# Second tile of a fused retention and expert kernel: the fifth block's transposes between the fourth block's two output passes, VectorE's fence, later weight sums and another order of PSUM banks

## The chip, the cores and the metric

The kernel runs on one core of a Trainium2 chip. The metric is the device time of one execution in microseconds; the times of before are three executions with a median of 293.08 us (292.98 to 293.34).

## The reference

Inputs are q, k and v of shape 8 x 8 x 576 x 64 (batch, head, position, width), and two weight matrices of 512 x 2048 and 2048 x 512. Cut to what matters:

```python
scores = np.matmul(q, k.transpose(0, 1, 3, 2)) / np.sqrt(64)
gamma = 1.0 - 2.0 ** (-5.0 - np.arange(8))           # one per head
rel = pos[:, None] - pos[None, :]
ret = scores * np.where(rel >= 0, gamma ** rel, 0.0)
x = np.matmul(ret, v)                                # to 4608 tokens x 512
h = x @ w_in
out = (h * np.cos(h)) @ w_out                        # 4608 x 512, float32
```

## The kernel before

**Blocks and tiles.** The 4608 tokens are 18 blocks of 256. Two blocks make a tile of 512 tokens, so there are nine tiles, n = 0 to 8. The second tile (n = 1) holds blocks 2 and 3; in the code a block is `j`, counted from 0. So the "fourth block" of the title is j = 3 and the "fifth" is j = 4.

**The retention part of a block.** GpSimd scales q and k by powers of gamma (`prep`, line 203, tile `qks`) and rounds v (`round_v`, line 214, tile `vb`). TensorE transposes q and k (`turned`, line 239), and ScalarE or VectorE copies the two transposed halves to SBUF (line 245, tile `qkT`). TensorE makes the scores (`scores`, line 332), VectorE masks them (line 341, tile `ret`). TensorE sums the states (`sums_of`, line 365), VectorE adds them up (line 416), and ScalarE rounds them (line 425, tile `sb`). Then `outputs(j, bank)` makes the block's slice of x in a PSUM tile `ov`: `out_own` multiplies masked scores by v in two passes (line 449), `out_carried` adds what comes from earlier states (line 477), and ScalarE copies the result to `xT` (line 496).

**The fence.** The two passes of `out_own` write the same PSUM regions from different halves of TensorE's rows. Between them stands either a drain of TensorE (no `guard` given) or a one-element copy on ScalarE that waits for the first pass and that the second pass waits for (line 464); in the second form TensorE does the work of `guard()` meanwhile.

**The expert part of a tile.** `mm1` does x times w_in in eight steps i = 0 to 7 for n = 1. A step is 16 matmuls of 128x256 into a PSUM tile `h` of one bank pair (line 525), a cosine on ScalarE into `cosh` (line 538, two buffers), and a multiplication on VectorE that reads both `h` and `cosh` and writes `gT` (line 539). A bank pair is free for its next user once that multiplication has read it. Below, "multiplication i" is the one of step i.

**PSUM.** There are three bank pairs `m`, `a`, `b`, and two single banks `n`, `st`. The string `banks_of[1]` names the pair of each of the eight steps. Other work takes pairs by tag.

**The second matmul.** It uses sums of quarters of the weights and of gT, seven products instead of eight (`product`, `mm2_seven`, line 640). Four sums of quarters of w_out are made once, on VectorE, in half tiles (`w_sums`, line 557); sum 7 is written over a quarter of `w_out_sb` itself. The sums of gT (`g_sum`, line 579) are made on VectorE and GpSimd. For n = 1 the first product (x = 1) is made early, right after the matmuls of step 3, and after a quarter of its 16 matmuls it calls `early()`, which is `outputs(3, ...)`.

**Order.** The schedule is by hand: each engine runs its instructions in the order in which the program emits them. `mm1` takes a table `inside` of work to emit ahead of its group of four matmuls with that number. In the second tile, steps 3 and 4 emit on VectorE: two half sums of weights (6 and 4), multiplication 3, two half sums (7), the copy of half of block 4's transposes, multiplication 4. GpSimd prepares blocks 4, 5 and 6 one after the other (`step`, emitted at steps 0 and 1).

Of the kernel before, what the change touches and what calls it, by code (L numbers as in the profile page):

```python
# [17 lines left out]
def kernel(  # L18
# [9 lines left out]
    nc = tc.nc  # L28
# [13 lines left out]
    E2 = ET // 2  # L42
# [387 lines left out]

    held = []

    def out_own(j, ps, guard=None):

        ret = tiles["ret", j]
        vb = tiles["vb", j]
        begun = set()
        gate = rest = None
        if chunks[j][0].pair:
            order = [(c, y) for c in chunks[j] for y in range(2)]  # L440
        else:
            order = [(c, c.y) for c in chunks[j]]
        for swap in (1, 0):
            for hg in range(0, HG, 2):
                for c, y in order:
                    he = c.half ^ swap
                    for h in (head(he, hg), head(he, hg + 1)):
                        part = (h % 2, he)
                        i = nc.tensor.matmul(  # L449
                            ov_cols(c, ps, h, c.n),  # L450
                            lhsT=vb[c.rows, y, h, :],
                            rhs=ret[c.rows, he, h % HG, y, :],
                            start=part not in begun,
                            stop=False,
                            skip_group_check=True,
                        )
                        if gate is not None:
                            after(i, gate)
                            gate = None
                        begun.add(part)  # L460
            if swap and guard is None:
                nc.tensor.drain()
            elif swap:
                gate = nc.scalar.copy(flag[:, 1:], flag[:, :1])
                after(gate, i)
                while held:
                    held.pop(0)()
                rest = guard()
        return rest or ()
# [19 lines left out]
            tiles["x", n] = xp.tile([P, DG, W], BF16, tag="xT", name="xT")  # L489
        return tiles["x", n][:, :, j % 2 * BK : j % 2 * BK + BK]  # L490

    def outputs(j, bank, guard=None):
        ps = psum.tile([P, DG, BK], F32, tag=bank, name="ov")
        rest = out_own(j, ps, guard)
        out_carried(j, ps)
        nc.scalar.copy(x_of(j), ps)  # L496
        for run in rest:
            run()
# [12 lines left out]
    def mm1(n, et, c0, w, bank, inside={}):  # L511
        if ("g", n) not in tiles:
            tiles["g", n] = gp.tile([P, ET, W], BF16, tag="gT", name="gT")
            tiles["g", n, "done"] = 0
        gT, xT = tiles["g", n], tiles["x", n]
        m = 1024 // w
        ps = psum.tile([P, m, w], F32, tag=bank, name="h")
        steps = [(j, dg) for j in range(m) for dg in range(DG)]
        in_parts = (n, et, c0) in ((0, 0, 0), (0, 4, 0))
        if in_parts:  # L520
            steps.sort(key=lambda u: u[1] // 2)
        for u, (j, dg) in enumerate(steps):
            if u % DG == 0 and u // DG in inside:
                inside[u // DG]()
            nc.tensor.matmul(  # L525
                ps[:, j, :],
                lhsT=w_in_sb[:, dg, (et + j) * P : (et + j + 1) * P],
                rhs=xT[:, dg, c0 : c0 + w],
                start=dg == 0 and not (in_parts and w < 512 and j % 2),
                stop=dg == DG - 1,  # L530
                skip_group_check=in_parts,
            )
            spread(n, w)
        if m in inside:
            inside[m]()

        cosh = cosp.tile([P, m, w], F32, tag="cosh", name="cosh")
        nc.scalar.activation(cosh, ps, ACTF.Sin, bias=half_pi, scale=1.0)  # L538
        nc.vector.tensor_mul(gT[:, et : et + m, c0 : c0 + w], ps, cosh)  # L539

    w_sum = {}
# [66 lines left out]
    def product(n, x, early=None):  # L608
        gT = tiles["g", n]
        parts = [(j, 0, N2) for j in range(2)]  # L610
        fold = n in (1, last)
        fresh = x not in ((6, 7, 3) if fold else (6, 7))
        if fresh:
            tag = {1: "n", 2: "st", 4: "m" if n == 1 else "st", 5: "st", 3: "n"}[x]
            if x == 5 and n == last:
                tiles["o", x] = [
                    psum.tile([P, c], F32, tag=t, name="o")
                    for t, c in (("b", N2), ("m", N2 // 2), ("a", N2 // 2))
                ]
            else:  # L620
                ps = psum.tile([P, 2, N2], F32, tag=tag, name="o")
                tiles["o", x] = [ps[:, j] for j in range(2)]
                tiles["all", x] = ps
        if x in (5, 3) and n == last:
            parts = [(0, 0, N2), (1, 0, N2 // 2), (1, N2 // 2, N2)]
        dst = tiles["o", x if fresh else 5 if x == 3 else 1]
        lhs = {1: gT[:, :E2, :256], 2: gT[:, E2:, :256], 4: gT[:, E2:, 256:]}.get(x)
        if lhs is None:
            lhs = tiles["gs", n, x]
        rhs = {1: w_quarter(0, 0), 2: w_quarter(1, 0), 3: w_quarter(1, 1)}.get(x)  # L630
        if rhs is None:
            rhs = w_sum[x]
        order = [(e, i) for e in range(E2) for i in range(len(parts))]
        if len(parts) > 2:
            order.sort(key=lambda u: u[1])
        for u, (e, i) in enumerate(order):
            if early and u == len(order) // 4:
                early()
            j, c0, c1 = parts[i]
            nc.tensor.matmul(  # L640
                dst[i],
                lhsT=lhs[:, e, j * P : (j + 1) * P],
                rhs=rhs[:, e, c0:c1],
                start=(fresh and e == 0 and (i == 0 or len(parts) > 2)),
                stop=(e == E2 - 1 and (i == len(parts) - 1 or len(parts) > 2)),
                skip_group_check=True,
            )
        return parts
# [279 lines left out]
        0: [(0, 0, BK), (0, BK, BK)] + [(et, 0, W) for et in range(4, ET, 2)],  # L928
        1: [(et, 0, BK) for et in range(0, ET, 4)] + [(et, BK, BK) for et in (8, 0, 12, 4)],
    }  # L930
    banks_of = {0: "mbambamb", 1: "mabmbmab", 2: "abmabmab"}

    adds, ps1 = [], []

# [17 lines left out]

    stores = []

    for n in range(NT):
        blocks = blocks_of.get(n) or [(e + k * E2, 0, W) for e in range(0, E2, 2) for k in range(2)]
        for i, (et, c0, cw) in enumerate(blocks):
            inside = {
                (0, 0): {2: block1_outputs},
                (1, 0): {2: lambda: w_sums(4, 0, 4), 4: lambda: states_and_scores(3, None, ("n", "st"))},  # L960
                (1, 1): {4: lambda: adds.append(sums_of(3, ("n", "st"))())},
                (1, 3): {1: lambda: (adds.pop()(), w_sums(6, 4, E2), w_sums(4, 4, E2))},
                (1, 4): {2: lambda: turned(4, ("st", "a"), (act, vec))},
                (1, 7): {2: lambda: turned(5, "m")},
                (2, 0): {1: lambda: adds.append(sums_of(6, ("n", "st"))())},
                (2, 1): {1: lambda: adds.pop()()},
                (2, 5): {1: lambda: turned(7, ("n", "st"))},
            }.get((n, i), {})
            mm1(n, et, c0, cw, banks_of.get(n, turn_of(n) * 3)[i], inside)
            if (n, i) == (1, 0):  # L970
                step(False)
                load_next()
            if (n, i) == (1, 1):
                step(False)
                for r0, ot in stores[3:] + stores[:3]:
                    stored_rows(r0, 0, DM, ot)
                load_next()
                step()
            if (n, i) == (1, 3):
                w_sums(7, 0, 4)  # L980
                w_sums(7, 4, E2)
                mm2_seven(1, {}, None, (1,), lambda: outputs(3, "a"))
            if n:
                sums_after(n, i)
            if n == 2 and i in (2, 4):
                for y in range(2):
                    scaled(nc.gpsimd, 8, "q" if i == 2 else "k", y)
            if (n, i) == (2, 6):
                round_v(8)
                prepared = 9  # L990
                load_next()
                load_next()
# [68 lines left out]
        def first_scores(flush, pend):  # L1061
            g_sum(n, 5, 4, E2)
            six = g_sum(n, 6, 4, E2)
            masks = scores(a, "a")
            add_a = sums_of(a, "b")
            add_b = sums_of(b, "m")
            masks[0]()
            add_a()()
            masks[1]()
# [5 lines left out]

        def next_scores(flush, pend):
            masks = []
            outputs(a, "a", lambda: masks.extend(scores(b, "b")))
            for masked in masks:
                masked()  # L1080
            tiles["rounded"]()
# [3 lines left out]
            pass  # L1085

        def last_outputs(flush, pend):
            outputs(b, "a", lambda: turned(6, "m", later=True))
            flush()

        def mid_unit(flush, pend):
# [61 lines left out]
```

## Time and profile before

| | |
|---|---|
| median of three runs | 293.08 us (292.98 to 293.34) |
| profiled execution, its time | 292.63 us |
| its span on the core | 290.9 us |
| TensorE matmul busy | 284.3 us, 98% of the span |
| VectorE, ScalarE, GpSimd busy | 75%, 59%, 51% |
| granted TensorE clock | 1.00 |

The span runs from the first to the last instruction of the profiled execution; 1.7 us of its time lie around it. Timeline rows give a start and a duration in microseconds from the start of the span, the engine, the source line, what is written and read, how many instructions are merged, and in brackets the idle time before them with what ended it. PE is TensorE's matmuls, PEld its weight loads, DVE VectorE, ACT ScalarE, POOL GpSimd.

### The profile page before, as it was taken

How to read it: one execution, taken by the hardware profiler on the slowest of the kernel's cores; microseconds unless marked ns; L12 is line 12 of the kernel's file. 1: busy time of each engine (PE TensorE's matmuls, PEld its weight loads, DVE VectorE, ACT ScalarE, POOL GpSimd, SP SyncE). 2: the span in 40 equal slices, each digit the busy share in tenths (PEclk: the TensorE clock that was granted, in tenths of full speed). 3: DMA queues.
4: the chain of work that ended last, by engine and by line, in shares of the span. 5: the costliest groups of instructions: out<-in, count | busy, mean ns of one | idle time of the engine just before them, and what ended most of it. 6: DMA issues, size and time to landing. Idle time of an engine off the chain costs nothing.

```text
span 290.9 us, 10529 instructions
## 1 busy us (share of the span) xinstructions
PE 284.3 (98%) x4336; PEld 191.3 (66%) x4336; DVE 218.5 (75%) x309; ACT 170.7 (59%) x200; POOL 147.9 (51%) x169
## 2 busy tenths in 40 slices
PE   7999999999999999999999999999999999999994
PEld 2664446888854786478647874687458845884584
DVE  5767758999967967896789677977698669745943
ACT  6756216756677655676467746673767476536620
POOL 7840435698977993379136923593348024002400
PEclk9999999999999999999999999999999999999999
DMA  7999999997997989837690589139101220122013
GB/s 218 275 171 205 252 235 247 224 220 195 223 224 183 268 207 230 210 78 176 170 227 15 129 200 217 42 99 231 38 0 41 65 49 0 41 51 59 0 38 108
DMA packets 103853, 42.62 MB, mean 146 GB/s; under 512 B 68480, under 2 KB 103296, under 8 KB 103808
## 3 DMA queue, kind: packets, MB, share of 16 engines
q1 hardware_dynamic: 99104, 37.37, 52.5%
q0 software_dynamic: 4256, 4.19, 9.1%
q8 instruction: 36, 0.59, 0.8%
q10 hardware_dynamic: 448, 0.39, 0.4%
q14 instruction: 9, 0.07, 0.1%
HBM read 36.70 MB, written 9.44 MB: 159 GB/s over the span
## 4 chain that ended last, share of the span: by engine, by line
PE 94%; DVE 3%; DMA 1%; issue 0%; ACT 0%; DVEq 0%; ACTq 0%
PE h L525 43%; PE o L640 34%; PE o L1025 5%; PE ov L449 3%; PE tr L239 3%; PE ov L477 2%; PE sc L332 2%; DVE ret L312 1%; PE st L365 1%; DMA fk<-in_k_dram 1%; DVE qks L171 1%; PE sc L299 0%; PE tr L260 0%; ACT ot L670 0%; PE idle L270 0%
## 5 line engine op out<-in xcount | busy, mean ns | idle before, releaser
L525 PE MATMUL h<-xT,w_in_sb 128*128 128x512 bf16 (+1 forms) x656 | 127.4, 353 | 0.0
L539 DVE TENSOR_TENSOR gT<-h,cosh 128x1024 bf16<-128x1024 f32 x72 | 87.8, 1221 | 27.3 <-ACT cosh L538 26.8
L538 ACT ACTIVATE cosh<-h,half_pi 128x1024 f32<-128x1024 f32 x72 | 80.2, 1115 | 40.7 <-PE h L525 40.7
L525 PEld LDWEIGHTS <-w_in_sb 128*128 128x128 bf16 x656 | 63.5, 98 | 58.6 <-DMA w_in_sb<-in_moe_w_in_dram 0.2
L579 POOL TENSOR_TENSOR gs<-gT 128x512 bf16<-128x512 bf16 x30 | 38.1, 1271 | 99.6 <-DVE gT L539 99.0
L640 PEld LDWEIGHTS <-gs 128*128 128x128 bf16 x528 | 49.6, 98 | 5.9
L203 POOL TENSOR_TENSOR qks<-fk,gkc 128x512 bf16<-128x512 f32 x32 | 39.0, 1237 | 5.1 <-DMA fk<-in_k_dram 5.1
L640 PEld LDWEIGHTS <-gT 128*128 128x128 bf16 x384 | 36.6, 98 | 6.1
L666 DVE TENSOR_TENSOR ot<-ot,o 128x512 f32<-128x512 f32 x35 | 23.3, 683 | 20.2 <-ACT ot L670 12.6
L245 ACT COPY qkT<-tr 128x1024 bf16<-128x1024 bf16 x29 | 27.7, 1021 | 12.0 <-PE tr L239 11.0
L203 POOL TENSOR_TENSOR qks<-fq,gq 128x512 bf16<-128x512 f32 x28 | 31.2, 1134 | 4.6 <-DMA fq<-in_q_dram 4.6
L640 PE MATMUL o<-w_out_sb,gs 128*128 128x256 bf16 (+1 forms) x264 | 30.7, 270 | 0.0
L640 PE MATMUL o<-w_out_sb,gT 128*128 128x256 bf16 x256 | 30.6, 273 | 0.0
L640 PE MATMUL o<-ws,gs 128*128 128x256 bf16 (+1 forms) x264 | 30.4, 269 | 0.0
L670 ACT COPY ot<-o 128x512 f32<-128x512 f32 x33 | 19.2, 586 | 18.1 <-PE o L640 17.5
L341 DVE TENSOR_TENSOR ret<-sc,mask_c 128x512 bf16<-128x512 f32 x32 | 20.6, 683 | 7.5 <-PE sc L332 6.6
L214 POOL CAST vb<-fv 128x512 bf16<-128x512 f32 x35 | 22.0, 650 | 6.7 <-DMA fv<-in_v_dram 6.7
L425 ACT CAST sb<-s_all 128x768 bf16<-128x768 f32 (+2 forms) x17 | 15.6, 919 | 14.0 <-DVE s_all L416 13.9
L416 DVE TENSOR_TENSOR s_all<-st,s_all 128x256 f32<-128x256 f32 x49 | 20.7, 422 | 1.9 <-PE st L365 0.6
L496 ACT CAST xT<-ov 128x1024 bf16<-128x1024 f32 x16 | 16.2, 1012 | 9.6 <-PE ov L477 9.4
L579 DVE TENSOR_TENSOR gs<-gT 128x512 bf16<-128x512 bf16 (+1 forms) x24 | 15.8, 660 | 0.6
L579 DVE TENSOR_TENSOR gs<-gs,gT 128x1024 bf16<-128x1024 bf16 x16 | 15.2, 948 | 0.3
(83 smaller groups left out, 213.7 us busy)
## 6 DMA issues: line engine op xcount, KB each, us to landing
out_dram<-ot SPq DMA_DIRECT2D x68, 128.0 KB, 2.7
fk<-in_k_dram SPq DMA_DIRECT2D x28, 256.0 KB, 5.3
fv<-in_v_dram SPq DMA_DIRECT2D x28, 256.0 KB, 4.8
fq<-in_q_dram SPq DMA_DIRECT2D x12, 512.0 KB, 5.0
w_out_sb<-in_moe_w_out_dram POOLq DMA_DIRECT2D x4, 512.0 KB, 9.6
fq<-in_q_dram SPq DMA_DIRECT2D x4, 384.0 KB, 7.3
fk<-in_k_dram SPq DMA_DIRECT2D x2, 512.0 KB, 5.0
fv<-in_v_dram SPq DMA_DIRECT2D x2, 512.0 KB, 5.9
```

Of the source, the lines that this page charges most:

```text
L203: return eng.tensor_tensor(out=dst.rearrange("p b a d -> p a b d"), in0=src.rearrange("p (a b) d -> p a b d", a=2), in1=by.rearrange("p (a ...
L214: runs[y](vb[:, y], f[:, :, y, :] if j < NP_B else f[:, y])
L245: lambda r=r: evacs[r](tiles["qkT", j][:, :, :, :, r * HP : r * HP + HP], pss[r])
L341: nc.vector.tensor_tensor(out=ret[:, he].rearrange("p b y i -> p (b y) i"), in0=ps[he].rearrange("p b y i -> p (b y) i"), in1=mask_c.unsqu ...
L416: nc.vector.tensor_tensor(out=s32[:, u], in0=ps[c.half][:, c.y], in1=s32[:, u - 1] if u else tiles["run"], op=ALU.add,)
L525: nc.tensor.matmul(ps[:, j, :], lhsT=w_in_sb[:, dg, (et + j) * P : (et + j + 1) * P], rhs=xT[:, dg, c0 : c0 + w], start=dg == 0 and not (i ...
L538: nc.scalar.activation(cosh, ps, ACTF.Sin, bias=half_pi, scale=1.0)
L539: nc.vector.tensor_mul(gT[:, et : et + m, c0 : c0 + w], ps, cosh)
L579: i = eng.tensor_tensor(out=tiles["gs", n, x][:, e : e + step], in0=a[:, e : e + step], in1=b[:, e : e + step], op=op_,)
L640: nc.tensor.matmul(dst[i], lhsT=lhs[:, e, j * P : (j + 1) * P], rhs=rhs[:, e, c0:c1], start=(fresh and e == 0 and (i == 0 or len(parts) > 2)),
L666: return lambda: nc.vector.tensor_tensor(out=out_, in0=in0, in1=in1, op=ALU.add)
L670: held.append(lambda ps=tiles["all", x]: nc.scalar.copy(t, ps))
```

## The change

All of it concerns the second tile (n = 1).

1. `outputs(3)` is given a guard: the 32 transposes of block 4, which stood in the middle of step 4, now stand between the two output passes, in place of the drain. The fence between the passes is a one-element copy on VectorE.
2. The early product, and with it `outputs(3)`, is emitted between the cosine and the multiplication of step 3. TensorE's order stays (matmuls of step 3, then the product); on VectorE the fence comes ahead of multiplication 3.
3. VectorE's copy of block 4's second transposed half, and after it the four half sums of weights (6, 4, 7, 7), are emitted after multiplication 3.
4. Step 4 goes from pair `b` to `m`, step 5 from `m` to `b`, step 7 from `b` to `m`. `outputs(3)` goes from `a` to `b`. The later users of `m` and `b` in this tile (block 5's and 6's transposes, product 4, two sums of states, the scores of block 5) change places with each other.

```diff
-    def out_own(j, ps, guard=None):
+    def out_own(j, ps, guard=None, fence=None):
...
             elif swap:
-                gate = nc.scalar.copy(flag[:, 1:], flag[:, :1])
+                gate = fence(flag[:, 1:], flag[:, :1])
...
-    def outputs(j, bank, guard=None):
+    def outputs(j, bank, guard=None, fence=nc.scalar.copy):
         ps = psum.tile([P, DG, BK], F32, tag=bank, name="ov")
-        rest = out_own(j, ps, guard)
+        rest = out_own(j, ps, guard, fence)
...
         nc.scalar.activation(cosh, ps, ACTF.Sin, bias=half_pi, scale=1.0)
+        if "cosine" in inside:
+            inside["cosine"]()
         nc.vector.tensor_mul(gT[:, et : et + m, c0 : c0 + w], ps, cosh)
...
-            tag = {1: "n", 2: "st", 4: "m" if n == 1 else "st", 5: "st", 3: "n"}[x]
+            tag = {1: "n", 2: "st", 4: "b" if n == 1 else "st", 5: "st", 3: "n"}[x]
...
-    banks_of = {0: "mbambamb", 1: "mabmbmab", 2: "abmabmab"}
+    banks_of = {0: "mbambamb", 1: "mabmmbam", 2: "abmabmab"}
...
+    def third_outputs():
+        def turn():
+            copies = turned(4, ("st", "a"), (act, vec), later=True)
+            adds.append(copies.pop())
+            return copies
+
+        outputs(3, "b", turn, vec)
...
-                (1, 3): {1: lambda: (adds.pop()(), w_sums(6, 4, E2), w_sums(4, 4, E2))},
-                (1, 4): {2: lambda: turned(4, ("st", "a"), (act, vec))},
-                (1, 7): {2: lambda: turned(5, "m")},
+                (1, 3): {
+                    1: lambda: adds.pop()(),
+                    "cosine": lambda: mm2_seven(1, {}, None, (1,), third_outputs),
+                },
+                (1, 7): {2: lambda: turned(5, "b")},
...
             if (n, i) == (1, 3):
-                w_sums(7, 0, 4)
+                adds.pop()()
+                for x in (6, 4, 7):
+                    w_sums(x, 4 if x < 7 else 0, 4 if x == 7 else E2)
                 w_sums(7, 4, E2)
-                mm2_seven(1, {}, None, (1,), lambda: outputs(3, "a"))
...
-            add_a = sums_of(a, "b")
-            add_b = sums_of(b, "m")
+            add_a = sums_of(a, "m")
+            add_b = sums_of(b, "b")
...
-            outputs(a, "a", lambda: masks.extend(scores(b, "b")))
+            outputs(a, "a", lambda: masks.extend(scores(b, "m")))
...
-            outputs(b, "a", lambda: turned(6, "m", later=True))
+            outputs(b, "a", lambda: turned(6, "b", later=True))
```

## The prediction

> **What bounds the kernel now.** I read the page first: TensorE is busy for 98% of the span, and the chain that ended last lies 94% on it. So a microsecond that TensorE loses or wins in the second tile is one of the end, unless TensorE waits later anyway; the view of waits puts only two waits down to its matmuls, 1.3 and 0.5 us in all.
>
> ```profile
> PE 284.3 (98%) x4336; PEld 191.3 (66%) x4336; DVE 218.5 (75%) x309; ACT 170.7 (59%) x200; POOL 147.9 (51%) x169
> PE 94%; DVE 3%; DMA 1%; issue 0%; ACT 0%; DVEq 0%; ACTq 0%
> ```
>
> Next the timeline of TensorE around the fourth block's outputs.
>
> ```profile
> 55.30 0.60 PE L640 MATMUL o<-w_out_sb,gT 128*128 128x256 bf16 x4
> 55.83 0.74 PE L449 MATMUL ov<-ret,vb 64*64 64x64 bf16 x32
> 56.39 0.43 PE L477 MATMUL ov<-qkT,sb 64*64 64x64 bf16 x32
> 56.75 1.48 PE L640 MATMUL o<-w_out_sb,gT 128*128 128x256 bf16 x12
> 58.07 1.04 PE L525 MATMUL h<-xT,w_in_sb 128*128 128x256 bf16 x8
> 59.04 0.64 PE L239 MATMUL tr<-ident,qks 64*128 64x64 bf16 x32
> 59.61 5.41 PE L525 MATMUL h<-xT,w_in_sb 128*128 128x256 bf16 x48
> 64.96 0.64 PE L239 MATMUL tr<-ident,qks 64*128 64x64 bf16 x32
> ```
>
> The step's 48 matmuls run from 59.61 to 64.96; less some 0.1 for the change of form, one is 0.1095 us. So step 4 ends at 60.49, step 5 at 62.24, step 6 at 63.99. Then the timelines of VectorE and GpSimd for the same stretch.
>
> ```profile
> 53.80 2.35 DVE L539 TENSOR_TENSOR gT<-h,cosh 128x1024 bf16<-128x1024 f32 x2
> 56.06 1.41 DVE L557 TENSOR_TENSOR ws<-w_out_sb,ws 128x1024 bf16<-128x1024 bf16 x2
> 57.39 1.22 DVE L539 TENSOR_TENSOR gT<-h,cosh 128x1024 bf16<-128x1024 f32 x1
> 58.52 2.85 DVE L557 TENSOR_TENSOR w_out_sb<-w_out_sb 128x1024 bf16<-128x1024 bf16 x2
> 61.30 0.68 DVE L245 COPY qkT<-tr 128x1024 bf16<-128x1024 bf16 x1
> 61.90 1.21 DVE L539 TENSOR_TENSOR gT<-h,cosh 128x1024 bf16<-128x1024 f32 x1
> 63.59 1.23 DVE L539 TENSOR_TENSOR gT<-h,cosh 128x1024 bf16<-128x1024 f32 x1 [0.48 <-ACT cosh L538]
> ```
>
> ```profile
> 57.22 2.15 POOL L203 TENSOR_TENSOR qks<-fq,gq 128x512 bf16<-128x512 f32 x2 [2.22 <-DMA fq<-in_q_dram]
> 59.34 2.94 POOL L203 TENSOR_TENSOR qks<-fk,gkc 128x512 bf16<-128x512 f32 x2
> 62.23 1.16 POOL L214 CAST vb<-fv 128x512 bf16<-128x512 f32 x2
> ```
>
> What the reader is to see: VectorE has no gap from 53.80 to 63.1. Two weight sums took 1.41 us together at 56.06, while GpSimd stood idle for fq; two of the same size took 2.85 at 58.52, beside GpSimd, whose second pair took 2.94 instead of the 2.04 that the same two take at 51.62. They take turns, one behind the other. Multiplication 4 ends at 61.90 + 1.21 = 63.11, and step 7, which uses its bank pair, begins at 63.99: a slack of 0.88 us.
>
> **The drain and the transposes (a gain).** Without a guard, 0.56 us lie from the first output pass to the carried part (55.83 to 56.39), and the transposes inside step 4 cost 0.57 plus the change of form of 0.1: 1.23 in all. The form that comes in their place stands in the trace at 77.69: first pass, 32 transposes at 77.94, second pass at 78.51, carried part at 78.66: 0.97. Gain 0.26 us.
>
> **The fence.** At 77.69 ScalarE's fence began 0.43 us behind the first pass's start and took 0.19; the second pass came 0.82 behind that start, so 0.2 are to spare. VectorE's one-element copy isn't in the trace; bounds are its memset of 128x1 (0.06) and ScalarE's 0.19, and below nothing is excluded, as it adds an instruction. Either hides behind the transposes, so nothing is put down for TensorE; if that cover were gone, 0.1 to 0.2. On VectorE, multiplication 3 is queued behind the fence, and behind that all else.
>
> **Bank b for outputs(3) (a loss).** Pair a had been released by multiplication 1 at about 55.0. Pair b is released by multiplication 2, which starts at 54.93 and ends at 56.15. From VectorE's end to a waiting matmul 0.05 us passed at 16.20 to 16.25 (ret L312 to ov L449). The first pass thus starts at 56.20 instead of 55.83: 0.37 lost (bounds 0.3 to 0.5). So TensorE has 56.20 + 0.97 for the passes + 0.36 for the carried part + 1.32 for the other 12 product matmuls = 58.85 for step 4, which now runs unbroken for 16 x 0.1095 = 1.75 to 60.60. That is 0.11 us later than before, and step 7 is due at 64.10.
>
> **VectorE's new order.** From 56.06:
> - The fence starts at 56.20 + 0.43 = 56.63. The cosine of step 3 (55.70, 1.12 long) ends at 56.82, so multiplication 3 goes from 56.87 and hands on at 58.0 (a step of 1.13 from one multiplication to the next, as 53.80, 54.93, 56.06).
> - The copy of transposes takes 0.60 to the next (61.30 to 61.90): 58.6. Its transposes are done by 57.0.
> - Four weight sums. Free of GpSimd they take 0.65 each (56.06 to 57.39): 61.2. All four in turns with it 1.46 each: 64.4. Row by row: GpSimd is in its second q instruction (58.34 to 59.34), then two of k, then two casts. The first sum meets what the sum of before met at 58.52, whose successor started at 59.85; the second ends like that one's successor, at 61.30. The third waits for the second k instruction, which ended at 62.28, then 0.6: 62.9. The fourth either follows at once (63.5) or lets one cast of 0.55 through (64.0). The nearest row is a cast at 69.93 that took 1.12 us, against 0.61 for its neighbour at 68.95, beside a sum of gT on VectorE at 69.88: casts take turns too. I take 64.0.
> - Multiplication 4 then runs from 64.0 to 65.2, against 61.90 to 63.11. Of the 2.1 us, 0.75 is VectorE's wait around the fence and 1.3 the two sums that had lain in GpSimd's idle time.
>
> The Trainium skill (SBUF — State Buffer, "Who interferes with whom") says that a VectorE instruction with two SBUF inputs and any GpSimd instruction that reads SBUF shut each other out for a whole instruction, the later one waiting. It speaks against this change: by it the fourth sum waits for a cast as well, as in my sum; were only GpSimd's two-input instructions shut out, the sum would be half a microsecond lower. The 2.85 against 1.41 us here agrees with it.
>
> **Who waits for multiplication 4.** Step 7, due at 64.10, gets pair m from it at 65.25: 1.15 lost. Half a step and the change of form (0.97) bring TensorE to block 5's transposes at 66.22; they need pair b, released by multiplication 5, which starts at 65.13 and ends at 66.35. So they start at 66.40 against 64.96: 1.44 us later in all. Block 5's transposes waited for multiplication 5 before too, in pair m; only its time has moved.
>
> **What costs nothing.** Step 4 in pair m needs multiplication 3 (58.1) by 58.85. Step 5 in b needs ScalarE's copy of x (about 57.6 to 58.6) by 60.6; step 6 in a needs the copied transposes (58.7) by 62.4. Product 4, both sums of states and the scores keep their predecessors under the other letter. At the tile's end block 6's transposes leave b instead of m: ScalarE's two copies end at 82.02, and the next tile's step 1 in b begins at 82.98, so 0.96 to spare. No DMA and no instruction of GpSimd is emitted elsewhere; GpSimd's casts are pushed by some 0.6 us and it has 0.67 idle before 64.06. Behind step 7 VectorE and ScalarE are as late as TensorE, so nothing gives the time back.
>
> **The sum.** Profiled time 292.63 + 0.11 + 1.15 + 0.18 = 294.07. The median of the runs is 0.45 above the profiled execution: 294.5.
>
> **Rivals.**
> - *The sums don't collide.* If they run at 0.65 each behind multiplication 3, multiplication 4 ends by 62.5, no step waits, and 0.11 remains: 293.2, no change. It decides from the point at which multiplication 4 ends before 64.1, so if the four sums together take under about 4.3 us. For it: GpSimd starts after a DMA, and a later fq moves the collision. Against it: GpSimd's five instructions stand back to back from 57.22 to 63.39. Chance 0.14.
> - *The gain alone.* If pair b comes free in time for 55.83 and the sums run free, the 0.26 is left, and with a cheaper switch of forms at most 0.6: 292.5 to 292.8. Against it: VectorE's queue up to multiplication 2 is untouched. Chance 0.10, half of it beyond 0.2%.
> - *Worse turns.* Each sum takes 1.53, the longest of the rows, and the fence holds the second pass by 0.2 besides: multiplication 4 ends at 65.9, the end is 2.2 us later: 295.3. Chance 0.08.
> - The forecast, 294.0 to 295.0: 0.68.
>
> **How the numbers follow.** The likeliest is 294.5. The range goes down to the first rival with its bounds (293.0) and up to 295.2; it leaves out the gain alone and most of the worst. About 0.2% (0.6 us) is what a measurement of this kernel can tell from no change. Slower by more: 0.68 + 0.08 and a little of the first rival, 0.78. Within: 0.16. Faster: 0.06.
>
> **What would show it.** In the profile of after: the first output pass starts at about 56.2 behind multiplication 2, with idle time ended by VectorE; no drain; the fence under the transposes; the four weight sums at a mean over 1.2 us, one after another from 58.6; multiplication 4 at about 64; a wait of TensorE of about 1.15 us before step 7 for line 539, and block 5's transposes at about 66.4. The prediction is wrong if the sums' mean is near 0.7, if step 7 starts by 64.3, or if TensorE's delay at block 5's transposes has shrunk by the next tile.

## The result and the profile after

The changed kernel takes 293.94 us (median of 15 runs, 292.65 to 295.23), the kernel before 292.98 (15 runs beside them, 292.28 to 293.98). The ratio is 1.0037 with a 95% interval of 1.0021 to 1.0053: slower by 0.6 to 1.6 us, about 1.0. The profiled execution took 293.94 us, with a span of 292.2.

Line numbers of the changed kernel are two higher from line 539 on: 541 is the multiplication, 559 the weight sums, 642 the second matmul, 581 the sums of gT. First TensorE's timeline, as it was shown for before:

```profile
55.55 0.60 PE L642 MATMUL o<-w_out_sb,gT 128*128 128x256 bf16 x4
56.45 0.32 PE L449 MATMUL ov<-ret,vb 64*64 64x64 bf16 x16 [0.30 <-DVE gT L541]
56.70 0.64 PE L239 MATMUL tr<-ident,qks 64*128 64x64 bf16 x32
57.27 0.32 PE L449 MATMUL ov<-ret,vb 64*64 64x64 bf16 x16
57.42 0.43 PE L477 MATMUL ov<-qkT,sb 64*64 64x64 bf16 x32
57.78 1.49 PE L642 MATMUL o<-w_out_sb,gT 128*128 128x256 bf16 x12
59.10 5.40 PE L525 MATMUL h<-xT,w_in_sb 128*128 128x256 bf16 x48
65.05 1.03 PE L525 MATMUL h<-xT,w_in_sb 128*128 128x256 bf16 x8 [0.54 <-DVE gT L541]
66.18 0.64 PE L239 MATMUL tr<-ident,qks 64*128 64x64 bf16 x32
...
67.64 1.91 PE L642 MATMUL o<-w_out_sb,gT 128*128 128x256 bf16 x16
```

Two brackets are new, and both name the multiplication: one before the first output pass (pair b, multiplication 2), one before step 7 (pair m, multiplication 4). The early product starts 0.25 us later than in the profile of before, ahead of anything that was changed: VectorE's scaling of block 3 waits for fq until 45.57 there, until 45.32 in before. So I measure by stretches. From the early product to product 2 it was 55.30 to 66.42 = 11.12 us before and is 55.55 to 67.64 = 12.09 now: 0.97 lost. From product 2 to the next tile's first matmul (80.78 before, 82.37 after) it was 14.36 and is 14.73. Then VectorE's and GpSimd's timelines:

```profile
54.05 2.35 DVE L541 TENSOR_TENSOR gT<-h,cosh 128x1024 bf16<-128x1024 f32 x2
56.82 0.15 DVE L464 COPY flag<-flag 128x1 f32<-128x1 f32 x1 [0.42 <-PE ov L449]
57.10 1.23 DVE L541 TENSOR_TENSOR gT<-h,cosh 128x1024 bf16<-128x1024 f32 x1
58.24 0.68 DVE L245 COPY qkT<-tr 128x1024 bf16<-128x1024 bf16 x1
58.84 2.13 DVE L559 TENSOR_TENSOR ws<-w_out_sb,ws 128x1024 bf16<-128x1024 bf16 x2
60.89 2.97 DVE L559 TENSOR_TENSOR w_out_sb<-w_out_sb 128x1024 bf16<-128x1024 bf16 x2
63.79 2.34 DVE L541 TENSOR_TENSOR gT<-h,cosh 128x1024 bf16<-128x1024 f32 x2
```

```profile
59.18 2.69 POOL L203 TENSOR_TENSOR qks<-fq,gq 128x512 bf16<-128x512 f32 x2 [1.00 <-DMA fq<-in_q_dram]
61.83 2.93 POOL L203 TENSOR_TENSOR qks<-fk,gkc 128x512 bf16<-128x512 f32 x2
```

VectorE is idle between multiplication 2 and the fence. The four weight sums follow in one row from 58.84 to 63.79, 4.95 us, beside GpSimd's four scalings of block 5, which are long too. Only then comes multiplication 4, at 63.79.

### The profile page after: what moved, and what is told of

Read it like the earlier page. It is cut to its first block, busy times and chain, and to the rows that moved or that the text cites. A ratio compares the mean times of both kernels' runs of the same rounds, so it can differ in the third digit from the quotient of the medians.

```text
span 292.2 us, 10509 instructions
## 1 busy us (share of the span) xinstructions
PE 283.1 (97%) x4315; PEld 191.2 (65%) x4336; DVE 219.6 (75%) x310; ACT 170.5 (58%) x200; POOL 148.4 (51%) x169
## 4 chain that ended last, share of the span: by engine, by line
PE 86%; DVE 7%; DMA 4%; ACT 1%; issue 1%; DVEq 0%; ACTq 0%
PE h L525 39%; PE o L642 34%; PE ov L449 3%; PE tr L239 3%; PE o L1038 3%; DMA fq<-in_q_dram 2%; DVE gT L541 2%; DVE ret L312 1%; PE sc L332 1%; PE ov L477 1%; DMA fk<-in_k_dram 1%; PE st L365 1%; ACT cosh L538 1%; DVE qks L171 1%; DVE w_out_sb L559 1%
```

## The experiments

Each kernel below the first two rows ran 12 times, but the one with GpSimd held only three times. Every ratio is against the kernel before run on the same chip beside it (median 293.29 us in the first four experiments, 293.03 in the next four, 292.91 in the last three). "First stretch" is from the early product to product 2, "second stretch" from there to the next tile, both in the profiled execution, of which there is one for each kernel; most times in the text are from it.

| kernel | median us | ratio, 95% interval | first stretch | second stretch |
|---|---|---|---|---|
| before | 292.98 | | 11.12 | 14.36 |
| changed | 293.94 | 1.0037 (1.0021 to 1.0053) | 12.09 | 14.73 |
| early sums | 292.84 | 0.9991 (0.9972 to 1.0010) | 11.22 | 14.36 |
| pair a | 293.86 | 1.0028 (1.0005 to 1.0051) | 12.27 | 14.37 |
| pair a, early sums | 292.72 | 0.9983 (0.9965 to 1.0000) | 10.95 | 14.36 |
| before, sums later | 294.59 | 1.0042 (1.0021 to 1.0062) | 12.90 | 14.82 |
| pair a, early sums, ScalarE's fence | 293.11 | 1.0000 (0.9978 to 1.0022) | 11.15 | 14.72 |
| before, early sums | 293.17 | 1.0005 (0.9987 to 1.0023) | 11.12 | 14.56 |
| changed, GpSimd held | 294.98 | 1.0062 (1.0036 to 1.0088) | 11.34 | 15.71 |
| pair a, early sums, other slot | 293.27 | 1.0001 (0.9985 to 1.0017) | 10.95 | 14.56 |
| pair a, early sums, GpSimd's order | 292.90 | 0.9994 (0.9977 to 1.0011) | 11.32 | 14.36 |
| before, GpSimd's order | 292.87 | 1.0000 (0.9980 to 1.0019) | 11.24 | 14.49 |
| changed, GpSimd's order | 293.93 | 1.0029 (1.0010 to 1.0048) | 12.14 | 14.36 |

### The weight sums made earlier

```diff
-                    (2, 5, 0), (8, 5, 4), (19, 6, 0),
+                    (2, 5, 0), (8, 5, 4), (19, 6, 0), (48.5, 6, 4),
...
-                (1, 0): {2: lambda: w_sums(4, 0, 4), 4: lambda: states_and_scores(3, None, ("n", "st"))},
+                (1, 0): {2: lambda: (w_sums(4, 0, 4), w_sums(4, 4, E2)), 4: lambda: states_and_scores(3, None, ("n", "st"))},
...
-                for x in (6, 4, 7):
-                    w_sums(x, 4 if x < 7 else 0, 4 if x == 7 else E2)
+                w_sums(7, 0, 4)
```

> The changed kernel, with the second halves of weight sums 6 and 4 made earlier: 6 in tile 0 while VectorE waits for fq (a gap of 0.69 us before 45.3), 4 in step 0 of the second tile behind its first half (a gap of 0.57 before 49.7). The same computation in another order. Theory (the sums behind multiplication 3, in turns with GpSimd, make multiplication 4 late, and step 7 waits for it): the two half sums that took 2.13 us at 58.84 are gone from there, multiplication 4 starts at 61.6 to 62.0, step 7 doesn't wait, block 5's transposes wait under 0.1; the wait of the first output pass for pair b stays at 0.3 to 0.4. Against the kernel before: +0.1 us (0.0 to +0.3). Rival (the loss is pair b's wait and VectorE's idle time around the fence; the sums don't matter): step 7 still waits 0.5 or more, and the loss stays at 0.7 to 1.0 us.

TensorE's and VectorE's timelines of that kernel:

```profile
56.59 0.32 PE L449 MATMUL ov<-ret,vb 64*64 64x64 bf16 x16 [0.31 <-DVE gT L541]
...
59.24 6.28 PE L525 MATMUL h<-xT,w_in_sb 128*128 128x256 bf16 x56
65.45 0.64 PE L239 MATMUL tr<-ident,qks 64*128 64x64 bf16 x32
```

```profile
58.97 2.20 DVE L559 TENSOR_TENSOR w_out_sb<-w_out_sb 128x1024 bf16<-128x1024 bf16 x2
62.34 1.23 DVE L541 TENSOR_TENSOR gT<-h,cosh 128x1024 bf16<-128x1024 f32 x1 [1.17 <-ACT cosh L538]
```

Step 7's half runs on from step 6 (56 matmuls in one row), and multiplication 4 now waits 1.17 us for its cosine instead of coming late. The wait for pair b stayed at 0.31. The first stretch is 11.22, 0.10 above before, where 0.11 had been the term for TensorE ahead of step 7. The loss is gone (interval from -0.8 to +0.3 us). The theory holds; the rival would have kept a wait before step 7.

### The output passes in pair a

```diff
-            copies = turned(4, ("st", "a"), (act, vec), later=True)
+            copies = turned(4, ("st", "b"), (act, vec), later=True)
...
-        outputs(3, "b", turn, vec)
+        outputs(3, "a", turn, vec)
```

> The changed kernel, with outputs(3) in pair a and the second half of block 4's transposes in pair b (the two letters change places). Theory: the first pass no longer waits for multiplication 2 (0.3 us of idle time gone; the transposes may wait up to 0.1), so step 7 is due about 0.3 us earlier; but multiplication 3 is held by its cosine and not by the fence, the sums behind it stand where they stood, multiplication 4 ends when it did, and step 7 waits 0.3 longer. Against the kernel before: +0.8 to +1.1 us, as the changed kernel. Rival (pair b's wait is a loss of its own that adds to the rest): 0.3 us of the loss are gone, +0.5 to +0.7 us.

TensorE's timeline, then VectorE's:

```profile
56.14 0.32 PE L449 MATMUL ov<-ret,vb 64*64 64x64 bf16 x16
...
65.29 1.03 PE L525 MATMUL h<-xT,w_in_sb 128*128 128x256 bf16 x8 [0.99 <-DVE gT L541]
```

```profile
56.52 0.15 DVE L464 COPY flag<-flag 128x1 f32<-128x1 f32 x1
57.16 1.23 DVE L541 TENSOR_TENSOR gT<-h,cosh 128x1024 bf16<-128x1024 f32 x1 [0.49 <-ACT cosh L538]
```

The first pass starts with no idle time, 0.53 us behind the early product as in before. But multiplication 3 waits for its cosine just the same, and step 7 waits 0.99 instead of 0.54. What was won in front is given back there: the first stretch is 12.27 against 12.09. So the two waits do not add up; the later one hides the earlier one. The ratio, 1.0028, fits that, but its interval (+0.15 to +1.5 us) would fit the rival's +0.5 to +0.7 as well: only the profile speaks against the rival.

### Both

The edits of the two kernels above together.

> Both edits of the two runs before. Theory: neither wait is left, and what remains is the gain of the drain and of the form change, 0.26 us less up to 0.1 for transposes that wait for pair b: -0.15 to -0.3 us against the kernel before. Rival (the drain in fact cost little, or VectorE's fence holds the second pass): 0.0 to +0.2 us, with idle time before the second pass.

```profile
59.08 6.28 PE L525 MATMUL h<-xT,w_in_sb 128*128 128x256 bf16 x56
```

The first stretch is 10.95, 0.17 below before: neither wait is left in it, and step 7's half follows step 6 in one row. The time is lower by 0.5 us, with an interval that ends at no difference. The theory's stretch is seen, the gain in time is not clear of zero.

### The sums alone, in the kernel before

```diff
-                (1, 3): {1: lambda: (adds.pop()(), w_sums(6, 4, E2), w_sums(4, 4, E2))},
+                (1, 3): {1: lambda: adds.pop()()},
...
             if (n, i) == (1, 3):
+                w_sums(6, 4, E2)
+                w_sums(4, 4, E2)
                 w_sums(7, 0, 4)
```

> The kernel before, with one part of the change alone: the half sums 6 and 4 emitted behind multiplication 3 (and before the two of 7). Drain, place of the transposes and bank pairs as before. Theory: multiplication 3 is at 56.9 (its cosine), the four sums take 4.9 to 5.4 us from 58.0 as they stand beside GpSimd, multiplication 4 ends at 64.7 to 65.2, step 7 (in pair b, which multiplication 4 releases) waits 0.6 to 1.2: +0.7 to +1.3 us against the kernel before. Rival (the loss comes from bank pair and fence): nothing, 0.0 to +0.2 us.

```profile
64.32 2.78 PE L525 MATMUL h<-xT,w_in_sb 128*128 128x256 bf16 x24 [1.62 <-DVE qkT L245]
```

The later place of the sums is enough to make the kernel of before slower, by 0.6 to 1.8 us. The place where it hurts was a miss: VectorE's copy of the transposes stands behind the sums in this kernel, so step 6, which needs pair a from that copy, waited 1.62 us before step 7 could wait for anything. The change avoids that by putting the copy ahead of the sums.

### ScalarE's fence

```diff
-        outputs(3, "a", turn, vec)
+        outputs(3, "a", turn)
```

on top of both edits.

> The kernel with pair a and the early sums, but the fence between the two output passes on ScalarE instead of VectorE. Theory (VectorE's fence is needed since ScalarE is busy with the cosine of step 3, which ended at 57.32 in that run): the fence ends at about 57.5, the second pass starts 0.3 us later than with VectorE's fence (57.25), and the gain is gone: -0.1 to +0.3 us against the kernel before, 0.25 to 0.35 us longer from the early product to product 2 than with VectorE's. Rival (any engine's fence hides behind the transposes): no difference between the two, -0.2 to -0.5.

Here the cosine of step 3 ran from 55.96 to 57.08 and the fence behind it from 56.97 to 57.16; the second pass began at 57.21, 1.12 us behind the first, against 0.92 (56.33 to 57.25) with VectorE's fence. The first stretch is 11.15 against 10.95: 0.20 longer, less than expected, and the stretch's gain over before is gone. The times of the two kernels (ratios 1.0000 and 0.9983) can't be told apart.

### Early sums without the rest

The early sums put into the kernel before.

> The kernel before with the second halves of sums 6 and 4 made early (tile 0 and step 0) and nothing else changed. Theory: before, no wait of TensorE hung on VectorE in this stretch, so relieving VectorE of 1.4 us there brings nothing: 0.0, between -0.2 and +0.2 us, and 11.1 us from the early product to product 2 as before. Rival (the early sums by themselves carry what the kernel with both edits gained): -0.3 to -0.6 us.

11.12 us for the first stretch, to the hundredth as in before, and a ratio of 1.0005. Multiplication 4 waits 1.13 us for its cosine there. VectorE's relief is worth nothing without the change; it only pays the change's debt.

### GpSimd held

The changed kernel, with GpSimd's preparation of block 5, and what stands behind it, made to wait for the last weight sum:

```diff
             if (n, i) == (1, 1):
-                step(False)
...
-                load_next()
-                step()
             if (n, i) == (1, 3):
...
-                w_sums(7, 4, E2)
+                step(False, w_sums(7, 4, E2))
...
+                load_next()
+                step()
```

`step`'s second argument is what block 5's first scaling waits for.

> The changed kernel, with GpSimd's preparation of block 5 (and all of GpSimd's work behind it) held until the last half sum of weights is done, so that the four sums run beside an idle GpSimd. Theory (the sums are long because they take turns with GpSimd): the four take 0.65 us each, 2.6 in all instead of 4.95, multiplication 4 starts as soon as its cosine is there (about 62.2), step 7 doesn't wait; GpSimd's four instructions start at about 61.5 and end at 65.6, so block 5's transposes wait up to 0.5 us for them. Rival (the sums are long of themselves, two of them since they write over the weights): 5 us in all as in the changed kernel, multiplication 4 at 63.8, step 7 waits 0.5 or more.

```profile
60.17 1.41 DVE L562 TENSOR_TENSOR ws<-w_out_sb,ws 128x1024 bf16<-128x1024 bf16 x2
61.50 1.29 DVE L562 TENSOR_TENSOR w_out_sb<-w_out_sb 128x1024 bf16<-128x1024 bf16 x2
63.51 1.23 DVE L544 TENSOR_TENSOR gT<-h,cosh 128x1024 bf16<-128x1024 f32 x1 [0.73 <-ACT cosh L541]
...
63.02 2.04 POOL L203 TENSOR_TENSOR qks<-fq,gq 128x512 bf16<-128x512 f32 x2 [3.64 <-DVE w_out_sb L562]
```

The same four sums in the same place take 2.6 us instead of 4.95 when GpSimd is idle, the two that write over the weights no longer than the others. Multiplication 4 waits for its cosine, step 7 for nothing, and the first stretch is 11.34. The whole kernel is slower than before all the same (1.0062). Its second stretch is 1.35 longer, since GpSimd is now late with everything behind: TensorE's second matmul is idle for 0.65 us, waiting for GpSimd's sums of gT. So GpSimd can't simply be put off. The profiled execution, at 295.61 the slowest of the three, also lost 1.59 us ahead of the early product, where nothing was edited: there VectorE waited 1.80 us for the load of the weights, until 38.34. That part says nothing of the edit.

### Another slot, and GpSimd's order

> The kernel with pair a and the early sums, and the half sum 6 emitted still earlier in tile 0, ahead of the states of block 2, where VectorE had 1.05 us idle (41.0 to 42.1) and GpSimd was idle too. Theory: that half sum takes 0.7 instead of 1.09 us and block 3's scaling on VectorE starts as soon as its fq is there; the second tile is as in the kernel with both edits: -0.2 to -0.5 us against the kernel before. Rival (the weights' last quarter has not landed by 41 us): VectorE waits there for a DMA, and the states of block 2 come later: 0.0 or slower.

This was half sum 6 at 42.5 instead of 48.5 in tile 0, on top of both edits; the number says after how many of that tile's matmuls of gT and w_out it is emitted. It waited 1.03 us for the weights' DMA, so the rival's cause was there: the sums of states came 0.45 later and block 2's outputs waited 0.26 for VectorE. The first stretch was 10.95 again, the time that of before.

In that kernel, as in some others, the second stretch was 0.2 to 0.5 longer than 14.36. In it GpSimd ended the second half of sum 7 of gT at 77.32, while product 7 had started at 75.95 and reads it in its second half: it took 1.98 instead of 1.85. So in three kernels I put that half sum ahead of GpSimd's two of sum 3:

```diff
-            g_sum(n, 3, 0, 4, gate=six)
-            seven = g_sum(n, 7, 0, 4)
+            g_sum(n, 7, 4, E2, gate=six, eng=nc.gpsimd)
+            g_sum(n, 3, 0, 4)
+            g_sum(n, 7, 0, 4)
...
-            g_sum(n, 7, 4, E2, gate=seven, eng=nc.gpsimd)
```

> The kernel with pair a and the early sums (half sum 6 at its first early place), and GpSimd's three sums of gT at the tile's end in another order: the second half of sum 7, which product 7 reads first, ahead of the two of sum 3; it no longer waits for VectorE's first half of sum 7. Theory (in the profiles of the kernels with early sums, product 7 waits 0.1 to 0.35 us for GpSimd whenever GpSimd's inputs came late, which eats the gain of 0.17): product 7 never waits, 14.36 us from product 2 to the next tile's first matmul, 10.95 from the early product to product 2: -0.3 to -0.6 us against the kernel before. Rival (GpSimd's order doesn't matter, what is left is scatter): -0.1, interval across zero.

> The kernel before with GpSimd's new order alone. Theory: in the profile of before product 7 did not wait (14.36 us from product 2 to the next tile), though GpSimd was only just in time, so only the executions with late inputs gain: -0.2 to 0.0 us, and 11.12 us from the early product to product 2. Rival (the order carries all that the kernel with all three edits wins): as much as that one.

> The changed kernel with GpSimd's new order alone. Theory: the 0.37 us that the profiled execution lost between product 2 and the next tile (14.73 against 14.36) are product 7 and the one behind it waiting for GpSimd and go away, the 0.97 of the first stretch stays: +0.5 to +1.0 us against the kernel before. Rival (that loss is also VectorE's, late since step 7): 14.6 to 14.8 us stay.

In the changed kernel the second stretch went from 14.73 to 14.36 and the first stayed (12.14), as the theory said; the time, 1.0029, is not separable from 1.0037. But that doesn't show that the order did it. In the execution with the old order two of TensorE's weight loads in this stretch came late:

```profile
78.45 0.33 PEld L642 LDWEIGHTS <-gs 128*128 128x128 bf16 x4 [0.18 <-POOL gs L581]
82.14 0.11 PEld L642 LDWEIGHTS <-gs 128*128 128x128 bf16 x2 [0.37 <-issue]
```

The first is product 7 waiting for GpSimd, which took 1.96 instead of 1.85: 0.11. The second is in the last product (2.03 instead of 1.76: 0.27), and "issue" means that it waited for nothing that the profile shows. GpSimd was also earlier in the execution with the new order: its last cast ahead of the sums of gT ended at 70.65, against 73.28 with the old one. And the kernel with pair a, which has the old order, had 14.37. So 0.11 of the 0.37 is GpSimd's, and what took it away is open. In the kernel before it was 14.49, where product 7 took 1.98 and the pass behind it waited for VectorE's masking, and there was no difference in time. With both edits, 14.36, but the first stretch was 11.32: the carried part (line 477) took 0.72 instead of 0.36, with a gap that the profile puts down to nothing. The time is that of before. No version beats the kernel before by more than the intervals allow.

## Why the prediction was right, and where it wasn't

**The wait for pair b: right.** The pass was due 0.53 behind the early product, at 56.08, and came at 56.45: 0.37, the number of the sum.

**The passes and the transposes: right.** From first pass to carried part 0.97 (56.45 to 57.42), as in the rows at 77.69, and 2.65 from the pass to step 4 (59.10), as in the sum.

**The fence: right in size.** It took 0.15 us, between the bounds of 0.06 and 0.19, and ended at 56.97, 0.3 before the second pass began (57.27). But the prediction booked 0.75 us of VectorE's delay as "VectorE's wait around the fence". The kernel with pair a shows that this was the wrong name: its fence came at 56.52, and multiplication 3 still waited 0.49 us for the cosine of step 3. The delay is what the removed sums leave open ahead of that cosine; the fence fills a part of it at no cost.

**The four sums: the mechanism right, the size too large.** Forecast 58.6 to 64.0, 5.4 us; measured 4.95. The row-by-row working took GpSimd's start, 57.22, from before, and let all four sums meet it. In the execution after, GpSimd began at 59.18, so the first sum ran alone (0.71 to the next) and three met it (1.34, 1.45, 1.45). The edits don't explain that late start, so it is chance: GpSimd was late with block 4 already, at 52.45 against 49.62, ahead of the edited place. A late start isn't even needed. In the changed kernel with GpSimd's other order GpSimd began at 57.66, but the first sum still came in just ahead of its second scaling of q: 5.0 us. In the kernel with pair a that scaling was first, all four sums met GpSimd (1.33, 1.33, 1.45, 1.02), and they took 5.13. Multiplication 4 came at 63.79, which is 63.54 on the clock of before. Hence step 7's wait: forecast 1.15, measured 0.69 (due at 59.10 + 48 x 0.1095 = 64.36, came at 65.05). The bounds for the end of the sums, 61.2 and 64.4, hold 63.54. That GpSimd causes the length was argued from 1.41 against 2.85 us; it is shown by the kernel with GpSimd held.

The fourth sum's wait for a cast did not occur in this execution, where the casts come after the sums. In the kernel with pair a it did: the last sum took 1.09 us instead of 0.68, and the two casts beside it 2.09 against 1.16 in before.

```profile
63.01 1.09 DVE L559 TENSOR_TENSOR w_out_sb<-w_out_sb 128x1024 bf16<-128x1024 bf16 x1
62.49 2.09 POOL L214 CAST vb<-fv 128x512 bf16<-128x512 f32 x2
```

By the Trainium skill (SBUF — State Buffer, "Who interferes with whom") a VectorE instruction with two SBUF inputs contends with any GpSimd instruction that reads SBUF, and so with a cast. The trace of that kernel agrees.

**Block 5's transposes: right.** Forecast 0.18 behind the 0.97 that follow step 7; measured 66.18 - 66.02 = 0.16.

**The sum.** 0.11 + 1.15 + 0.18 = 1.44 forecast; 0.12 + 0.69 + 0.16 = 0.97 for the first stretch in the profile. The term of step 7 alone was mis-sized, by 0.46. That 0.96 lies between the medians too is partly chance, for the rest of the profiled execution differs as well: 0.25 was lost ahead of the edits and 0.37 behind product 2, and 0.32 came back later, between the third tile's first matmul (82.37 against 80.78) and the ninth's (262.14 against 260.87). The 0.45 between profiled execution and median, which the forecast of 294.5 added, wasn't there either: both are 293.94.

**"Behind step 7 ... nothing gives the time back": right up to the next tile, but more was lost.** I had GpSimd's delay end in its idle time before 64.06. In the profile it didn't: GpSimd waited for fq until 66.43 before block 6, and its sums of gT ended at 80.63 instead of 79.08. The second stretch grew by 0.37, of which 0.11 is product 7's wait for GpSimd; the cause of the other 0.27 is open. How much of it is in the median is open too, and variants of the kernel before lose 0.1 to 0.5 us there as well. The 0.32 that came back later is no more than the third tile differs between the profiles of all these kernels (30.80 to 31.19 us from its first matmul to the fourth's), so it isn't shown to be a gain of the change.

**The first rival** came true by design in the kernel with early sums: once no sum holds multiplication 4, 0.10 is left of the loss and the time is that of before. Its price of 0.11 was right, its condition was not met by the change.

## What to carry to other kernels

Before a wait is taken from the busiest engine, ask which engine releases the next buffer, and walk that engine's queue instruction by instruction up to the release: here 0.17 to 0.26 us of drain and switching were bought with 1.6 us of delay on VectorE, of which step 7 paid 0.7. Work that is put behind an instruction "because it isn't urgent" can meet another engine there; the same sums cost 0.65 us each in a gap of GpSimd and up to 1.5 beside it. And where two waits lie in a row on one path, removing the first alone may bring nothing, as here: test both together before calling either harmless.

## What the runs showed of the hardware that I had not expected

The moment at which GpSimd begins decides who meets whom: its preparation of block 5 began anywhere from 57.13 to 59.18 us in the kernels that leave it in place, in most of them on the landing of fq. The same four sums behind multiplication 3 took 4.95 us in the changed kernel, 5.0 in it with GpSimd's other order, 5.13 with pair a and 5.3 in the kernel before with the sums later. A forecast from one profile's start of GpSimd is no better than that range. And one-element copies are not free: 0.15 us on VectorE and 0.19 on ScalarE, where VectorE's memset of the same size took 0.06.
